# Three small reorderings in a fused spectral-mix and gated-MLP kernel with its backward pass

## The chip, the cores and the metric

One core of one Trainium2 chip. The metric is device microseconds of one launch, median of several runs. A profiled execution of the same program stands beside the runs; all durations below are from it.

## The reference, cut to what matters

Forward, with x of 2048 x 576 in bf16, F = 4608:

```python
g = sigmoid((x * gate_w).sum(-1))
a = irfft2(rfft2(x) * (w_r + 1j * w_i))              # spectral branch, over (2048, 576)
b = (gelu(x @ w_gate) * (x @ w_up)) @ w_down         # MLP branch
out = g * a + (1 - g) * b
```

Computed are `out` and, by `jax.vjp` with a given `grad_out`, the gradients of `x`, `w_r`, `w_i`, `w_gate`, `w_up`, `w_down` and `gate_w`. In the reference `x` of the MLP branch is the same array as that of the spectral branch.

## The kernel before

The 2048 rows lie as 128 partitions x 16 row tiles `t`. F is cut into 18 groups `g` of 256 columns. The main part of the kernel is a loop over `g` and over four blocks `m` of four row tiles each: 72 steps, numbered `pr = 4g + m` from 0 to 71. One step does the following on TensorE (PE), in this order:

- `H_mm`: 20 matmuls of `z = grad_out @ w_down^T` (L444, L449), the short matmuls of gate and up (L453), and then `full(0)` and `full(1)` (L460), eight matmuls for each of two pairs of row tiles. Their results lie in PSUM: `z` in the only buffer of pool `pz`, `xy` in two buffers of pool `ph`.
- ScalarE (ACT) takes `z` out (`da`, L472), then for each `xy` a square and two casts (`H_act`, L479, L481, L482). VectorE (DVE) makes the elementwise products: `H_ew1` (L487 to L491) in the same step, `H_ew2` (L507 to L528, two of them ACT sigmoids) after the next step has begun, because `sigs()` is called at the end of a step. DVE takes its instructions in this order; L528 is the last of `H_ew2`.
- the weight-gradient products of the group before: `u_dw` (d_w_gate and d_w_up, L590, 16 matmuls of 512 columns), `u_dwd` (d_w_down, L572, 16 matmuls of 288 columns) and `tail` (L604). They accumulate in the two buffers of pool `pw` and are cut into jobs of 4 or 8 matmuls. `W_units` says which jobs go to which `m`. An ACT cast (`wevac`, L541) takes a finished product out, and POOL issues its store.
- FFT pieces. The spectral branch and its gradient are cut into 207 slots (some of them empty, `gap`), held in the list `fft` in a fixed order: 64 forward pieces (`u1`: L633, L636, taken out by ACT as `Y`; `u2`: L651, taken out by ACT as `ve`, then five DVE operations and a store by SP); a table and two turned tables; then, pair by pair of rows, four 32-point pieces `s2` (L752, taken out by L757) and four `s1` (L841, L844); and the inverse pieces `z`, `ztail` (L901) and `d` (L915, L917). In the lines the first of these is L888. Every piece writes PSUM tile `pf`, and `pf` is the same single buffer of `pz` that `z` of the step uses. So a piece's first matmul waits until the piece ahead of it has been taken out, and the next step's `z` waits for the last one.

How many pieces a step gets is fixed by `want(pr)`: for the first steps by the tuple `FIRST` (running totals), after it by a share that grows evenly until the pieces are used up in step 64. When a step has pieces and its number is over 6, the first of them goes between the two row tiles of `full(1)`, that is between the gate|up halves of `xy` (L1132, `between`); the others go among the weight-gradient jobs, at places that L1154 to L1158 choose by weight. Around the first piece only, `pcopy[0]` is VectorE's copy (`VC`) in place of ScalarE's (`AC`); inverse pieces already use `pcopy[0]`, 32-point pieces do not.

A piece `s2` fills two PSUM column blocks on 128 partitions. L757 takes it out in two copies of 64 partitions x 578 elements, one for the real part (c = 0, partitions 0 to 63) and one for the imaginary part (c = 1, partitions 64 to 127). When the fourth `s2` of a pair is out, the pair's products go on DVE as "side work", about 4.4 us by the kernel's own estimate in each step, behind `H_ew1`.

The order of `dB`: `dB` holds grad_out and is scaled in place by 1 - g in four parts of four row tiles (`scale_dB`): part 0 and 2 (ACT) and 1 (DVE) in and right after step 4, part 3 (ACT, L1042) at the start of step 5's `xy`, behind the casts of two products. d_w_down uses all 16 row tiles of `dB`: its first half (`f(0)`) row tiles 0 to 7, its second row tiles 8 to 15.

After the 72 steps (from about 951 us) a second part multiplies the stored intermediates by the weights (L1276); it takes no FFT piece.

Of the kernel before, what the change touches and what calls it, by code (L numbers as in the profile page):

```python
# [19 lines left out]
S, D, DF = 2048, 576, 289  # L20
# [25 lines left out]
def eo(c):  # L46

    return slice(c, 512, 4)
# [227 lines left out]
def kernel(  # L276
# [4 lines left out]
    nc = tc.nc  # L281
# [258 lines left out]
    def wevac(out, in_):  # L540
        wcopy[0](out, in_)  # L541
# [3 lines left out]
    def dwtile(name):  # L545
        if not spare:
            return stage.tile([P, 2, FG], BF16, tag="dw", name=name)
        spare.append(spare.pop(0))
        return ew.tile([P, 4, FG], BF16, tag=spare[-1], name=name, bufs=2)[:, 0:2, :]

    def W_units(g):
        fsl = slice(g * FG, (g + 1) * FG)
        kt = kept[g]

        def tl(k, t):
            tile_ = kt[t // 4][min(k, 1)]
            return tile_[:, t % 4, :] if k == 0 else tile_[:, t % 4, k - 1, :]
        dwd_tiles, wp = {}, {}

        def halves(f, us):  # L560
            return [(us, lambda: f(0)), (us, lambda: f(1))]

        def wtile(key):
            if key not in wp:
                wp[key] = pw.tile([P, TPB, FG], F32, tag="wps", name="wps")
            return wp[key]

        def u_dwd(fch, h):
            def f(half):
                wps = wtile(("d", fch, h)).rearrange("p a b -> p (a b)")  # L570
                for t in range(8 * half, 8 * half + 8):
                    nc.tensor.matmul(wps[:, :288], lhsT=tl(0, t)[:, fch * P:(fch + 1) * P],  # L572
                                     rhs=dB[:, t, h * 288:(h + 1) * 288], start=(t == 0), stop=(t == T - 1))
                if half == 0:
                    return
                if h == 0:
                    dwd_tiles[fch] = stage.tile([P, D], BF16, tag="dwd", name="dwd")
                dwd = dwd_tiles[fch]
                wevac(dwd[:, h * 288:(h + 1) * 288], wps[:, :288])
                if h == 1:  # L580
                    r0 = g * FG + fch * P
                    wst[0].dma_start(out_6[r0:r0 + P, :], dwd[:])
            return halves(f, 1.0)

        def u_dw(c, cuts=(0, 4, 8, 12, T)):

            def f(t0, t1):
                wps = wtile(("w", c))
                for t in range(t0, t1):
                    nc.tensor.matmul(wps[:].rearrange("p a b -> p (a b)"), lhsT=xn[:, t, c * P:(c + 1) * P],  # L590
                                     rhs=kt[t // 4][1][:, t % 4].rearrange("p k f -> p (k f)"), start=(t == 0), stop=(t == T - 1))
                if t1 < T:
                    return
                dw = dwtile("dw")
                wevac(dw[:], wps[:])
                for k, ov in enumerate((o4v, o5v)):
                    wst[0].dma_start(ov[:, c, fsl], dw[:, k, :])  # L597
            return [(3.45 * (b - a) / T, lambda a=a, b=b: f(a, b)) for a, b in zip(cuts, cuts[1:])]

        def tail():  # L600
            wps = wtile("t")
            for t in range(T):
                for k, r in ((1, LO), (2, HI)):
                    nc.tensor.matmul(wps[r, 0, :], lhsT=xn[:, t, 512:576], rhs=tl(k, t),  # L604
                                     start=(t == 0), stop=(t == T - 1))
            dw = dwtile("dwt")
            wevac(dw[:, 0], wps[:, 0, :])
            wst[0].dma_start(out_4[512:576, fsl], dw[LO, 0, :])
            wst[0].dma_start(out_5[512:576, fsl], dw[HI, 0, :])
        w = [u_dw(c, (0, 12, T)) if g == 0 and c < 2 else u_dw(c) for c in range(4)]  # L610
        d = [u_dwd(fch, h) for fch in range(FCH) for h in range(2)]
        if g == 0:
            return [[w[0][:1], w[1][:1]], [d[0], d[1]], [d[2], d[3], w[2][:2]], [w[2][2:], w[3][:2]], w[3][2:], {1: [w[0][1][1], w[1][1][1]], 2: [tail]}]
        return [[d[0]], [d[1], d[2], d[3]], [w[0], w[1][:2]], [w[1][2:], w[2]], w[3], {2: [tail]}]


# [5 lines left out]
    def pftile(dt=F32):  # L622
        return pz.tile([P, 2, 512 if dt is F32 else 1024], dt, tag="z", name="pf")
# [99 lines left out]
    def mid_units():  # L723
# [13 lines left out]
        def prefetch(p):  # L737
            st[p, "vx"] = load_V(scr_x, p)
            st[p, "vg"] = load_V(scr_g, p)
            w = unit([2, 2, DF], name="Wt")  # L740
            for k, v in enumerate((A_w_r, A_w_i)):
                for sb, d in rows(w[:, k], v, p):
                    ST.dma_start(sb, d)
            st[p, "w"] = w

        def s2(p, which, j):
            def f():
                Vp = st[p, "v" + which]
                xps = pftile()
                for t in range(2):  # L750
                    g = 2 * t + j
                    nc.tensor.matmul(xps[:, t, :DF], lhsT=tb.B[:, int(p == 0 and g == 0), :], rhs=Vp[:, g, :], start=True, stop=True)  # L752
                if j == 0:
                    st[p, which] = unit([2, 2, DF], name="X" + which)
                o = st[p, which]
                for c in range(2):
                    nc.scalar.copy(o[64 * j:64 * j + 64, :, c, :], xps[64 * c:64 * c + 64, :, :DF])  # L757
                if which == "g" and j == 1:
                    side.extend(products(p))
                    if p == 0:  # L760
                        prefetch(p + 1)
            return f
# [176 lines left out]
    VC, AC = V.tensor_copy, nc.scalar.copy  # L939
    pcopy = [AC]  # L940
# [5 lines left out]
    for c in range(6):  # L946
        w = gwr[0:1, eo(c)] if c < 4 else gwr[0:1, 512:D]
# [57 lines left out]
    mid_at = 4 * T + 10  # L1005
    NPR = NT // 2
    LASTP = NG * NPR - 7
    FIRST = (0, 0, 0, 0, 0, 0, 1, 5)
    done = [0]

    def want(pr):

        n0 = FIRST[-1]
        if pr < len(FIRST):
            return FIRST[pr]

        def load(n):

            return n + 0.5 * min(max(n - mid_at, 0), n_mid)
        share = load(n0) + (load(n_slots) - load(n0)) * (pr + 1 - len(FIRST)) / (LASTP - len(FIRST))  # L1020
        n = n0
# [24 lines left out]
    for g in range(NG):  # L1046
# [3 lines left out]
        for m in range(NPR):  # L1050
# [128 lines left out]
            if done[0] == n_slots or (pr >= wgT_from and pr % 2 == 0 and len(wgT_all) < 20):  # L1179
                load_wgT()  # L1180
                if done[0] == n_slots:
                    load_wgT()
        carry = pend[4] if pend else []
        pend = W_units(g)
    flush()
    assert fft_pos[0] == len(fft) and not side
# [239 lines left out]
```

## Time and profile before

| | |
|---|---|
| median of 4 runs | 1382.4 us (1381.2 to 1383.38) |
| the profiled execution, its own time | 1381.46 us |
| its span, first to last instruction | 1379.7 us |
| VectorE busy | 781.7 us (57% of the span) |
| ScalarE busy | 701.5 us (51%) |
| L757, ScalarE, 64 copies | mean 637 ns |
| L655, ScalarE, 32 copies of `ve` | mean 660 ns |
| step 7 (81.06 to 93.03 us) | ScalarE busy 10.93 of 11.97 us |
| step 35 (447.67 to 460.34 us) | VectorE busy 10.71 of 12.67 us |

The starts of the steps are the first L444 matmul of each. Times in the text are microseconds from the span's start, or from the start of a step where that is said. A matmul's end in the profile is a model: while TensorE runs without a break, a matmul starts before the end of the one ahead of it, so lost time is read from the distance of two starts.

### The profile page before, as it was taken

The numbers are of one execution on the slowest core, as the hardware profiler recorded it, in microseconds if no ns is written. First come the engines' busy times: TensorE is split into PE (matmuls) and PEld (weight loads), VectorE is DVE, ScalarE is ACT, GpSimd is POOL, SyncE is SP. The second block draws the span as 40 slices with busy tenths as digits, with TensorE's granted clock in tenths as the row PEclk, the third lists the DMA queues.
The fourth block names the chain that finished last, engine by engine and source line by source line (L and its number), as shares of the span: only waits on it lengthen the run. The fifth ranks groups of instructions, "written<-read, shape, count | busy, mean of one in ns | idle before, by whom it ended". The sixth has DMA issues, their size and how long they took to land.

```text
span 1379.7 us, 25988 instructions
## 1 busy us (share of the span) xinstructions
PE 1363.3 (99%) x10187; PEld 910.0 (66%) x10272; DVE 781.7 (57%) x1514; ACT 701.5 (51%) x1300; POOL 262.8 (19%) x513
## 2 busy tenths in 40 slices
PE   9999999999999999999999999999999999999999
PEld 7556656566556556556656566556777777777777
DVE  7887777765988877885676766650002642122101
ACT  7887777768878777866766767651000000000000
POOL 6211111132445444331111111110000110000000
PEclk9999999999999999999999999999999999999999
DMA  7425444456566556555556656759999997788774
GB/s 234 128 86 148 123 125 120 128 163 157 133 161 167 154 159 164 132 155 150 138 155 154 166 153 162 178 126 284 196 193 202 217 193 170 154 162 164 159 149 88
DMA packets 512423, 218.94 MB, mean 159 GB/s; under 512 B 312011, under 2 KB 503181, under 8 KB 512301
## 3 DMA queue, kind: packets, MB, share of 16 engines
q1 hardware_dynamic: 495178, 191.89, 59.9%
q0 software_dynamic: 14912, 24.24, 6.2%
q8 instruction: 80, 1.31, 0.4%
q10 hardware_dynamic: 2210, 1.15, 0.3%
q14 instruction: 43, 0.34, 0.1%
HBM read 45.51 MB, written 98.30 MB: 104 GB/s over the span
## 4 chain that ended last, share of the span: by engine, by line
PE 94%; ACT 2%; DVE 2%; issue 1%; POOL 0%; ACTq 0%; DVEq 0%; POOLq 0%
PE acc L1276 31%; PE wps L590 17%; PE xy L460 17%; PE wps L572 10%; PE z L444 8%; PE wps L604 2%; PE xy L453 2%; PE z L449 2%; PE pf L633 1%; PE pf L915 1%; PE pf L841 1%; PE pf L752 1%; PE pf L917 1%; PE pf L651 1%; PE pf L636 1%
## 5 line engine op out<-in xcount | busy, mean ns | idle before, releaser
L1276 PEld LDWEIGHTS <-pin 128*128 128x128 bf16 x3456 | 338.0, 98 | 85.8 <-issue 0.5
L590 PE MATMUL wps<-dH,xn 128*128 128x512 bf16 x1136 | 270.0, 379 | 0.9
L460 PE MATMUL xy<-wgu,xT 128*128 128x512 bf16 x1083 | 258.4, 379 | 8.3 <-issue 7.0
L460 PEld LDWEIGHTS <-xT 128*128 128x128 bf16 x1152 | 106.4, 98 | 132.9 <-issue 24.8
L590 PEld LDWEIGHTS <-xn 128*128 128x128 bf16 x1152 | 111.5, 98 | 118.5 <-issue 0.6
L1293 ACT COPY bo<-acc 128x288 f32<-128x288 f32 x32 | 12.8, 399 | 305.0 <-PE acc L1276 305.0
L572 PE MATMUL wps<-dB,A 128*128 128x288 bf16 x1152 | 153.4, 286 | 0.1
L597 POOL DMA_DIRECT2D out_dram<-dw x134 | 72.8, 547 | 408.4 <-ACT dw L541 368.1
L1276 PE MATMUL acc<-wgT,pin 128*128 128x288 bf16 x1152 | 143.8, 286 | 0.0
L1276 PE MATMUL acc<-wuT,pin 128*128 128x288 bf16 x1152 | 143.6, 286 | 0.0
L1276 PE MATMUL acc<-wd_all,pin 128*128 128x288 bf16 x1152 | 142.6, 286 | 0.0
L444 PE MATMUL z<-wdT,dOT 128*128 128x256 bf16 x1152 | 137.7, 273 | 0.1
L572 PEld LDWEIGHTS <-A 128*128 128x128 bf16 x1152 | 112.1, 98 | 32.8 <-issue 0.3
L472 ACT ACTIVATE da<-z,omg 128x256 bf16<-128x256 f32 x288 | 112.0, 471 | 31.9 <-PE z L449 31.8
L444 PEld LDWEIGHTS <-dOT 128*128 128x128 bf16 x1152 | 112.4, 98 | 21.7 <-issue 0.6
L1348 DVE SCALAR_TENSOR_TENSOR f32t<-gwf,dlog,b16t 128x576 f32<-128x576 f32 x16 | 13.1, 818 | 173.3 <-DMA b16t<-dxa_scr 173.3
L481 ACT CAST xb<-xy 128x512 bf16<-128x512 f32 x144 | 85.0, 591 | 48.4 <-PE xy L460 48.4
L479 ACT ACTIVATE q<-xy 128x512 bf16<-128x512 f32 x144 | 88.0, 613 | 14.6 <-PE xy L460 13.3
L482 ACT CAST hu<-xy 128x512 bf16<-128x512 f32 x144 | 87.4, 607 | 0.0
L518 DVE TENSOR_TENSOR xb<-xb,sg 128x1024 bf16<-128x1024 bf16 x48 | 33.1, 690 | 84.8 <-ACT sg L510 84.7
L541 ACT CAST dw<-wps 128x512 bf16<-128x512 f32 x72 | 42.3, 590 | 55.5 <-PE wps L590 53.4
L1307 DVE SCALAR_TENSOR_TENSOR b16t<-b16t,g,f32t 128x576 bf16<-128x576 bf16 x16 | 13.1, 818 | 96.1 <-DMA b16t<-a_scr 95.8
(239 smaller groups left out, 1703.0 us busy)
## 6 DMA issues: line engine op xcount, KB each, us to landing
scr<-dH SPq DMA_DIRECT2D x144, 256.0 KB, 3.3
scr<-A SPq DMA_DIRECT2D x72, 256.0 KB, 2.5
out_dram<-dw POOLq DMA_DIRECT2D x134, 64.0 KB, 2.5
wd_all<-in_B_w_down_dram SPq DMA_DIRECT2D x3, 1728.0 KB
out_dram<-dwd POOLq DMA_DIRECT2D x34, 144.0 KB, 2.9
scr_p<-Vt SPq DMA_DIRECT2D x32, 145.0 KB, 2.5
wgu<-in_B_w_gate_dram SPq DMA_DIRECT2D x18, 256.0 KB, 4.3
wgu<-in_B_w_up_dram SPq DMA_DIRECT2D x18, 256.0 KB, 3.4
```

The source lines that it names most:

```text
L444: nc.tensor.matmul(zo(t), lhsT=dOT[:, ci, t, :], rhs=wdT[:, ci, :], start=(t % 4 < 2 and ci == 0), stop=False)
L460: nc.tensor.matmul(xy[k][:, t % 2, :], lhsT=xT[:, ci, t, :], rhs=wgu[:, ci, :], start=False, stop=(ci == 3))
L472: nc.scalar.activation(da[:, t, :], z[:, t % 2, t // 2, :], ACT.Copy, scale=omg32[:, 4 * m + t:4 * m + t + 1])
L479: nc.scalar.activation(q[:, h, :], xy[:, :, 0:FG], ACT.Square)
L481: nc.scalar.copy(xb[:, h, :], xy[:, :, 0:FG])
L482: nc.scalar.copy(hu[:, h, :], xy[:, :, FG:2 * FG])
L518: V.tensor_tensor(xb[:], xb[:], s[:], op=ALU.mult)
L541: wcopy[0](out, in_)
L572: nc.tensor.matmul(wps[:, :288], lhsT=tl(0, t)[:, fch * P:(fch + 1) * P], rhs=dB[:, t, h * 288:(h + 1) * 288], start=(t == 0), stop=(t == ...
L590: nc.tensor.matmul(wps[:].rearrange("p a b -> p (a b)"), lhsT=xn[:, t, c * P:(c + 1) * P], rhs=kt[t // 4][1][:, t % 4].rearrange("p k f -> ...
L597: wst[0].dma_start(ov[:, c, fsl], dw[:, k, :])
L1276: nc.tensor.matmul(acc[:, :288], lhsT=src[:, r, :], rhs=w_of(r)[:, h * 288:(h + 1) * 288], start=(first and r == 0), stop=(last and r == F ...
```

## The change

```diff
@@ W_units: jobs of group 0, by m
-            return [[w[0][:1], w[1][:1]], [d[0], d[1]], [d[2], d[3], w[2][:2]], ...
+            return [[w[0][:1], w[1][:1]], [d[0][:1], d[1][:1], d[0][1:], d[1][1:]], [d[2], d[3], w[2][:2]], ...
@@ s2: the 32-point piece
-                for c in range(2):
-                    nc.scalar.copy(o[64 * j:64 * j + 64, :, c, :], xps[64 * c:64 * c + 64, :, :DF])
+                for c, cp in enumerate((AC, pcopy[0])):
+                    cp(o[64 * j:64 * j + 64, :, c, :], xps[64 * c:64 * c + 64, :, :DF])
@@ pieces done after each of the first steps
-    FIRST = (0, 0, 0, 0, 0, 0, 1, 5)
+    FIRST = (0, 0, 0, 0, 0, 0, 1, 4, 7)
```

First, step 5, which runs the first two d_w_down products, does both first halves and then both second halves. Second, a 32-point piece that stands between the gate|up halves has its imaginary part copied by VectorE and its real part by ScalarE; elsewhere both stay on ScalarE. Third, steps 7 and 8 get three FFT pieces in place of four. As the totals after them are computed anew, the pieces of most steps up to step 60 move by one or two places: after step 8 seven pieces are done instead of nine, the totals are the same again for good from the end of step 60, and step 64 ends the list in both. No matmul is added or removed.

In the changed program 12 of the 32 `s2` pieces are the first piece of their step (steps 25, 26, 27, 30, 32, 33, 35, 36, 38, 39, 41 and 44). In steps 7 and 8 the order of TensorE's matmuls becomes, by line and count (without L444 to L453; L633 and L636 are one `u1`, L651 is one `u2`):

```
step 7 before  L460x12 u1 L460x4 L590x4 u2 L590x4 u1 L590x4 u2 L590x4
step 7 after   L460x12 u1 L460x4 L590x4 u2 L590x8 u1 L590x4
step 8 before  L460x12 u1 L460x4 L590x4 u2 L590x4 u1 L572x8 u2 L572x8
step 8 after   L460x12 u2 L460x4 L590x4 u1 L590x4 L572x8 u2 L572x8
```

More of the change, by code (lines that the diff above doesn't have):

```diff
@@ L612, in W_units @@
         if g == 0:
-            return [[w[0][:1], w[1][:1]], [d[0], d[1]], [d[2], d[3], w[2][:2]], [w[2][2:], w[3][:2]], w[3][2:], {1: [w[0][1][1], w[1][1][1]], 2: [tail]}]
+            return [[w[0][:1], w[1][:1]], [d[0][:1], d[1][:1], d[0][1:], d[1][1:]], [d[2], d[3], w[2][:2]], [w[2][2:], w[3][:2]], w[3][2:], {1: [w[0][1][1], w[1][1][1]], 2: [tail]}]
         return [[d[0]], [d[1], d[2], d[3]], [w[0], w[1][:2]], [w[1][2:], w[2]], w[3], {2: [tail]}]
```

## The prediction

> **What bounds the kernel now.** I read the page's busy times first, then the chain that ended last, TensorE's waits, and the timeline around each wait.
>
> ```profile
> PE 1363.3 (99%) x10187; PEld 910.0 (66%) x10272; DVE 781.7 (57%) x1514; ACT 701.5 (51%) x1300; POOL 262.8 (19%) x513
> ...
> PE 94%; ACT 2%; DVE 2%; issue 1%; POOL 0%; ACTq 0%; DVEq 0%; POOLq 0%
> ```
>
> TensorE (PE) is the bound from start to end, and the change adds and removes no matmul. So only time in which PE stands still can move. PE's own list of waits names what the change can reach:
>
> ```profile
> PE pf L633 <- ACT ve L655: 0.9, 2, 0.6
> PE pf L752 <- ACT Xg L757: 0.5, 1, 0.5
> ```
>
> (Total, times, longest.) Both are the single `pf` buffer: a piece waits until ScalarE has taken out the one ahead. The list hides waits shorter than the modelled end of a matmul, so I measure lost time by distances of starts. Undisturbed, four L590 matmuls take 0.86 us to the next start, eight take 1.72, eight L572 take 0.98. Step 7, from the timeline (start, duration, engine, line, operation; in brackets the idle time before it and what ended it), first TensorE's rows, then one of ScalarE's:
>
> ```profile
> 87.64 1.03 PE L590 MATMUL wps<-dH,xn 128*128 128x512 bf16 x4
> 88.50 0.41 PE L651 MATMUL pf<-Y,Rt 128*128 128x292 bf16 x2
> 88.75 1.02 PE L590 MATMUL wps<-dH,xn 128*128 128x512 bf16 x4
> 90.42 0.42 PE L633 MATMUL pf<-Dt,xT 128*128 128x146 bf16 x4 [0.64 <-ACT ve L655]
> ...
> 89.66 0.70 ACT L655 COPY ve<-pf 128x584 f32<-128x584 f32 x1
> ```
>
> The first two rows give 0.86. From 88.75 to 90.42 it is 1.67: 0.81 lost, because ScalarE, busy almost without a break since 77.6, reaches `ve` at 89.66 only. TensorE goes on at 90.42, 0.06 after the copy's end. The same reading over steps 5 to 71:
>
> - step 5: 32 L572 matmuls last 4.37; 16 last 2.12 and 16 more 1.96, so 0.29 lost. The second half of the first d_w_down product waits for the last part of `dB` (ScalarE L1042, 62.03 to 64.84; TensorE goes on at 64.89).
> - step 7: 0.81, and 0.09 before its last `u2`; step 8: 0.39 (100.71 to 101.96 with four L590).
> - step 35: eight L590, 455.95 to 458.37, 2.42 against 1.72: 0.69. Steps 26, 38, 44: 0.2 each.
> - steps 14, 18, 54, 59: 0.14, 0.26, 0.09, 0.14, lone places where four L590 are too short a cover for a copy. Steps 13, 16, 18, 19, 22: together 0.6, which stay.
>
> That is 4.1 us in all, the ceiling of any gain.
>
> **The change part by part, costed on TensorE.**
>
> (1) *d_w_down by halves.* No instruction more. The first half of the second product (8 x L572, 0.98 us) now covers the wait of 0.29. Its PSUM buffer is free by 62.2 (L541 casts, 61.09 to 62.18), before its start at about 63.7. Both products still finish at the step's end and are cast in the same place. **-0.3.** ScalarE, late in steps 5 to 7, does not eat this gain: in step 6 it waits for TensorE itself (0.36 us before its cast at 77.57), so all after it starts earlier too.
>
> (2) *One piece less in steps 7 and 8.* Step 7: between the first `u2` and the next `u1` now stand eight L590, 1.72 us, and `ve` is out 1.67 after their start: no wait. The last `u2` and its 0.09 leave. Step 8: order u2, u1, u2. Its first copy keeps ScalarE's place of `Y` (99.00, 0.67), the `u1` follows, and behind it stand four L590 and eight L572, 1.84 us, over a copy of 0.65. **-0.8 - 0.1 - 0.4 = -1.3.** The moved pieces' 0.4 to 0.7 us of matmul are paid in later steps. Each carries its DVE work (2.0 us for a `u2`, into steps with 2 to 4 us of idle VectorE) and one SP store a step later (2.2 us to landing). The table, the loads `Vp` (5.3 to 5.9 us) and POOL's twelve `Wt` issues (0.5 us each) shift with them. The first 32-point piece moves from 317.6 to about 325 and its loads from about 297 to about 305, some 20 us ahead of use: no cost, and one only if more than 14 us of that cover went.
>
> (3) *32-point copies.* ScalarE loses 12 copies of 0.64. VectorE gets 12 of 64 x 578 from PSUM, of which the trace has none. Bounds: VectorE's cast of 288 elements, 0.45, and of 1024, 1.22. I take 0.76, the nearest row (L925, 580 elements, 757 ns). In the changed program VectorE's copy waits for ScalarE's counter alone, so it stands behind the ScalarE half, not beside it. It also stands behind L528 on VectorE. Behind it wait `H_ew1` and the side work; nothing on TensorE needs these soon (`dH` is read a group later). Step 35:
>
> ```profile
> 453.79 1.28 ACT L757 CAST Xx<-pf 64x578 bf16<-64x578 f32 x2
> ...
> 454.28 0.69 DVE L528 TENSOR_TENSOR dH<-dH,sg 128x1024 bf16<-128x1024 bf16 x1
> ...
> 455.70 0.41 PE L752 MATMUL pf<-Vp,Btab 128*128 128x289 bf16 x2
> ...
> 457.01 1.31 ACT L757 CAST Xg<-pf 64x578 bf16<-64x578 f32 x2
> ...
> 458.37 0.41 PE L752 MATMUL pf<-Vp,Btab 128*128 128x289 bf16 x2 [0.52 <-ACT Xg L757]
> ```
>
> ScalarE's half ends at 454.43, L528 at 454.97, VectorE's half at 455.73; TensorE wants 455.70 and gets 455.79: +0.09. In return ScalarE's next copies end 0.64 earlier, 457.68, just as TensorE wants them: -0.69. Steps 26 and 44 likewise (-0.2 each); in 38 the next piece gets 12 L590 of cover (-0.2). At 0.45 the 0.09 is gone. At 1.22 it is 0.55, and step 39 could lose as much, 1.0 more in all. In the other ten steps L528 ends 6.3 to 7.8 after the step's start and the next piece is wanted at 8.0 to 9.9, so 0.76 fits. **-1.2.**
>
> A copy of 580 elements out of PSUM takes 757 ns on VectorE (L925) and 658 on ScalarE (L923). The Trainium skill, "Perfetto Trace Analysis", section "Optimizing Scalar/DVE Operations", has a rule that speaks against this part: VectorE's access overhead is about 125 ns on PSUM, ScalarE's about 51. The trace agrees in sign. By the page a moved copy would take, as an estimate, 0.07 us more than ScalarE's, and the sum would differ by under 0.1, since only step 35 has no slack.
>
> (4) *The shifted schedule, steps 14 to 60.* Gone with their neighbours: 0.14 + 0.26 + 0.09 + 0.14 = -0.6. New short covers, read from the new order:
> - step 21 becomes like step 13 (u1, then u2 after eight L572, then u1): 166.45 to 167.58 against 0.98, +0.15; step 17 about +0.05.
> - step 52 puts a `d` four L590 after a wide `z`. As in step 60 the `z` copy (1.01) would start 0.65 after the first L888, at 771.05, and end at 772.06; the `d` would be wanted at 770.85 + 0.86 = 771.71: +0.41.
> - step 60 starts with a `z` copied by VectorE, and the `d` follows after four L590, not eight as in step 56:
>
> ```profile
> 723.71 0.69 DVE L528 TENSOR_TENSOR dH<-dH,s 128x1024 bf16<-128x1024 bf16 x1
> 724.32 1.22 DVE L891 CAST ZT<-pf 128x1024 bf16<-128x1024 f32 x1
> ...
> 724.35 1.89 PE L590 MATMUL wps<-dH,xn 128*128 128x512 bf16 x8
> ```
>
> Wanted at 724.35 + 0.86 = 725.21, free at 725.54 + 0.06: +0.39. Together **-0.6 + 1.0 = +0.4.** I add 0.3 for short covers I may have missed (two of the kind of step 13).
>
> Sum: -0.3 - 1.3 - 1.2 + 0.4 + 0.3 = **-2.1 us**. The profiled execution took 1381.46 (span 1379.7, 1.76 around it) and would take 1379.4; it lies 0.94 below the median of the runs shown, to which I apply the same difference: 1382.4 - 2.1 = **1380.3 us**.
>
> **The rivals.**
> - *Full gain.* Every wait named goes, and the new ones of (4) are hidden (a copy starting earlier because ScalarE runs ahead): -0.3 - 1.3 - 1.3 - 0.6 = -3.5, 1378.9 us. For it: ScalarE idles 2 to 5 us in steps 52 and 60. Against it: those waits are one copy's own length, which idle time doesn't shorten.
> - *Only moved.* The pieces pushed out of steps 7 and 8 make as many short covers as they leave: the new schedule has seven steps with five pieces (13, 17, 21, 52, 56, 60, 64), the old one six, one of them with empty slots. Then -0.3 - 1.3 - 1.2 is answered by some 2.5 of new waits: 1382.1 us. For it: fifteen steps lost time before, 0.1 to 0.9 each, at places that the weights in the source do not tell.
> - *VectorE late (slower).* In steps 28, 29, 33 and 43 VectorE idles 0.4 to 0.6 us of 12 to 13, and in step 28 L528 ends 8.06 after the start. If its queue were that late in all 12 steps, TensorE would stand (8.06 + 0.76 + 0.06 - 8.04) = 0.84 in each: +10.1, with the rest 1382.4 - 2.1 + 10.1 = 1390.4. It decides once these waits add up to more than 2.1, that is from 0.18 a step. Against it: step 28 itself starts with an `s1`, and the 12 steps have L528 at 6.1 to 7.8.
>
> **How the numbers follow.** Forecast 0.56, full gain 0.24, only moved 0.14, VectorE late 0.06. The forecast's own range is 1379.3 to 1381.3 (the unknown copy's 1.0 upwards, (4)'s 1.0 of new waits downwards). For 8 in 10 I take 1378.3 to 1382.7: full gain and only-moved included, with the runs' own spread about a median; VectorE late is left out. 0.2%, about what a measurement of this kernel can tell from no change, is 2.8 us: faster means below 1379.6, slower above 1385.2. Full gain is faster, and a little of the forecast's lower end (0.05): 0.29. Slower is VectorE late, 0.06. The rest, 0.65, is within.
>
> **What would show it.** Right: `pf L633 <- ACT ve L655` gone from TensorE's waits, no L572 row in step 5 ending late, step 35's last L752 0.7 us nearer the one ahead; L757 on VectorE x12 of about 0.76 us; new waits at L915 in steps 52 and 60. Wrong: L752 waiting on VectorE for over 0.2 us in several steps, waits of `pf` on a DMA, or the second part of the kernel (from about 951) changing its length.

## The result and the profile after

The changed kernel takes 1379.43 us (median; before in the same comparison 1381.32). The ratio is 0.9987, 95% interval 0.9982 to 0.9991: 1.9 us or 0.14% less. The interval leaves out 1, so the kernel is faster, but by less than the 0.2% that the prediction took for the bound of "faster". The spans of the profiled executions differ by 2.1 us (1379.7 to 1377.6): 2.04 in the part from step 5 to the second part, 0.19 in the part ahead of it, which varies from execution to execution, and 0.14 the other way behind the last matmul. The absolute number, 1380.3, was 0.9 too high because it hung on a median of four runs; the median of many lies 1.1 us lower.

The page of after, its busy times and its chain:

```profile
PE 1361.7 (99%) x10186; PEld 909.2 (66%) x10272; DVE 789.0 (57%) x1526; ACT 694.3 (50%) x1288; POOL 262.2 (19%) x513
...
PE 95%; DVE 2%; DMA 1%; issue 1%; ACT 0%; ACTq 0%; SPq 0%; DVEq 0%
```

TensorE is still the bound; ScalarE lost 7 us of work and VectorE took as much. TensorE's list of waits in after (total, times, longest):

```profile
PE xy L460 <- issue: 7.0, 44, 0.2
...
PE pf L915 <- ACT ZT L891: 0.2, 1, 0.2
PE pf L915 <- DVE ZT L891: 0.2, 1, 0.2
```

The two `pf` rows of before (L633 and L752) are gone, and two new ones stand at L915. (A third new row, L415 with 0.6, lies at about 6 us, ahead of the first step.) Step 7 in the timeline of after (start, duration, engine, line, operation):

```profile
88.02 0.41 PE L651 MATMUL pf<-Y,Rt 128*128 128x292 bf16 x2
...
88.27 1.89 PE L590 MATMUL wps<-dH,xn 128*128 128x512 bf16 x8
...
89.19 0.70 ACT L655 COPY ve<-pf 128x584 f32<-128x584 f32 x1
...
90.00 0.42 PE L633 MATMUL pf<-Dt,xT 128*128 128x146 bf16 x4
```

From 88.27 to 90.00 it is 1.73, the undisturbed length of eight L590: the 0.81 is gone. The copy ends at 89.89, 0.11 before the next piece starts. The eight L590 are the *cover* of that copy: the matmuls that run while the buffer is being emptied. In step 8 a new wait stands:

```profile
100.99 0.41 PE L651 MATMUL pf<-Y,Rt 128*128 128x292 bf16 x2
...
101.24 1.14 PE L572 MATMUL wps<-dB,A 128*128 128x288 bf16 x8
...
101.78 0.65 ACT L655 COPY ve<-pf 128x584 f32<-128x584 f32 x1 [0.98 <-PE pf L651]
...
102.47 1.80 PE L444 MATMUL z<-wdT,dOT 128*128 128x256 bf16 x15
```

Eight L572 give 0.98 to the next start, and the next step's `z` comes after 1.23: 0.25 lost. The copy starts 0.79 after L651 did; where ScalarE is idle, its other copies start 0.45 to 0.5 after. VectorE's copies, from the view of the line L757 (duration min/median/max in ns, first and last start):

```profile
L757 ACT CAST Xx<-pf x27: 635/637/639, 323.9 to 558.2; 64x578 bf16<-64x578 f32 x27
L757 ACT CAST Xg<-pf x25: 635/637/638, 328.9 to 569.0; 64x578 bf16<-64x578 f32 x25
L757 DVE CAST Xg<-pf x7: 754/762/764, 339.3 to 566.0; 64x578 bf16<-64x578 f32 x7
...
L757 DVE CAST Xx<-pf x5: 754/762/764, 324.6 to 527.3; 64x578 bf16<-64x578 f32 x5
```

Twelve copies of 0.762, against 0.76 taken. The Trainium skill, "Perfetto Trace Analysis", "Optimizing Scalar/DVE Operations", agrees in sign, but the row gives a difference of 0.125 us to ScalarE's copy where its figures gave an estimate of 0.07. Those figures are busy times; the same section puts the profiled latency at about twice them, and by that the estimate would be 0.15. Step 35 in after:

```profile
451.59 0.64 ACT L757 CAST Xx<-pf 64x578 bf16<-64x578 f32 x1
...
451.72 0.69 DVE L528 TENSOR_TENSOR dH<-dH,sg 128x1024 bf16<-128x1024 bf16 x1
...
452.33 0.75 DVE L757 CAST Xx<-pf 64x578 bf16<-64x578 f32 x1
...
453.64 0.41 PE L752 MATMUL pf<-Vp,Btab 128*128 128x289 bf16 x2
...
453.84 0.58 ACT L541 CAST dw<-wps 128x512 bf16<-128x512 f32 x1 [0.16 <-PE wps L590]
453.89 1.89 PE L590 MATMUL wps<-dH,xn 128*128 128x512 bf16 x8
...
454.45 1.28 ACT L757 CAST Xx<-pf 64x578 bf16<-64x578 f32 x2
...
455.78 0.41 PE L752 MATMUL pf<-Vp,Btab 128*128 128x289 bf16 x2
```

VectorE's half stands behind L528, as said, and is out at 453.08, 0.56 before the second L752: no wait there. The third L752 comes 1.89 after the eight L590 began (455.78 - 453.89): 0.17 lost. Between the second piece and its copies ScalarE makes the cast L541 of a finished product. Step 26 has the same order on ScalarE, and the next step's `z` comes 0.17 late:

```profile
342.67 0.58 ACT L541 CAST dw<-wps 128x512 bf16<-128x512 f32 x1 [0.44 <-PE wps L590]
...
343.28 1.28 ACT L757 CAST Xx<-pf 64x578 bf16<-64x578 f32 x2
```

And step 60:

```profile
775.36 0.69 DVE L528 TENSOR_TENSOR dH<-dH,s 128x1024 bf16<-128x1024 bf16 x1
...
775.97 1.22 DVE L891 CAST ZT<-pf 128x1024 bf16<-128x1024 f32 x1
776.00 1.03 PE L590 MATMUL wps<-dH,xn 128*128 128x512 bf16 x4
...
777.23 0.22 PE L915 MATMUL pf<-Dt,ZT 128*128 128x145 bf16 x1 [0.21 <-DVE ZT L891]
```

1.23 for four L590 of 0.86: 0.37 lost, where 0.39 had been worked out.

The time lost on TensorE, by distances of starts, in us (steps 13, 16, 19, 22 and the second place of 18 keep their 0.07 to 0.16):

| place | before | foreseen | after |
|---|---|---|---|
| 5, second half of d_w_down | 0.29 | 0 | 0 |
| 7, `u1` behind `ve` | 0.81 | 0 | 0 |
| 7, last piece | 0.09 | 0 | 0.09 (ahead of step 8's `z`) |
| 8 | 0.39 | 0 | 0.25 (ahead of step 9's `z`) |
| 14, 18, 54, 59 | 0.63 | 0 | 0 |
| 21; 17 | 0 | 0.15; 0.05 | 0.16; 0 |
| 26; 38; 44 | 0.2 each | 0 | 0.17; 0; 0 |
| 35 | 0.69 | 0.09 | 0.17 |
| 52; 60 | 0 | 0.41; 0.39 | 0.40; 0.375 |
| all of these | 3.5 | 1.1 + 0.3 for missed ones | 1.6 |

The measure for all that follows is the *stretch* from the first L444 of step 5 to the first L1276: 896.73 us before, 894.68 after, -2.04 (-1.89 in the table, the rest at places under 0.05). Equal stretches of TensorE's work repeat within 0.01 us between executions: steps 61 to 70 do in before and after, and the second part takes 424.66 from its first to its last matmul in all twelve profiles. The part ahead of step 5, which waits for loads, varies by up to 0.5, and what follows the last matmul takes 3.40 to 3.56, 0.14 more in after than in before; why is not known. The prediction had named a change of the second part's length as a sign against itself; on TensorE there is none. That is how a difference can be read that the times don't resolve, though each stretch is read from one profiled execution.

### The profile page after: what moved, and what is told of

It reads as the page before. It is cut to its first block, busy times and chain, and to the rows that moved or that the text cites. A ratio compares the mean times of both kernels' runs of the same rounds, so it can differ in the third digit from the quotient of the medians.

```text
span 1377.6 us, 25978 instructions
## 1 busy us (share of the span) xinstructions
PE 1361.7 (99%) x10186; PEld 909.2 (66%) x10272; DVE 789.0 (57%) x1526; ACT 694.3 (50%) x1288; POOL 262.2 (19%) x513
## 4 chain that ended last, share of the span: by engine, by line
PE 95%; DVE 2%; DMA 1%; issue 1%; ACT 0%; ACTq 0%; SPq 0%; DVEq 0%
PE acc L1276 31%; PE wps L590 18%; PE xy L460 17%; PE wps L572 10%; PE z L444 8%; PE wps L604 2%; PE xy L453 2%; PE z L449 2%; DMA wgu<-in_B_w_up_dram 1%; PE pf L633 1%; PE pf L915 1%; PE pf L651 1%; PE pf L752 1%; DMA xn<-in_A_x_dram 1%; PE pf L917 1%
## 5 line engine op out<-in xcount | busy, mean ns | idle before, releaser
L1276 PEld LDWEIGHTS <-pin 128*128 128x128 bf16 x3456 | 338.0, 98 | 85.8 <-issue 0.5
L590 PE MATMUL wps<-dH,xn 128*128 128x512 bf16 x1135 | 269.6, 379 | 1.0
L460 PE MATMUL xy<-wgu,xT 128*128 128x512 bf16 x1083 | 258.3, 379 | 8.3 <-issue 7.0
L460 PEld LDWEIGHTS <-xT 128*128 128x128 bf16 x1152 | 106.4, 98 | 132.6 <-issue 24.8
L590 PEld LDWEIGHTS <-xn 128*128 128x128 bf16 x1152 | 111.7, 98 | 119.0 <-issue 0.6
L572 PE MATMUL wps<-dB,A 128*128 128x288 bf16 x1152 | 153.7, 286 | 0.0
L1276 PE MATMUL acc<-wgT,pin 128*128 128x288 bf16 x1152 | 143.8, 286 | 0.0
L1276 PE MATMUL acc<-wuT,pin 128*128 128x288 bf16 x1152 | 143.6, 286 | 0.0
L1276 PE MATMUL acc<-wd_all,pin 128*128 128x288 bf16 x1152 | 142.6, 286 | 0.0
L444 PE MATMUL z<-wdT,dOT 128*128 128x256 bf16 x1152 | 137.7, 273 | 0.1
L572 PEld LDWEIGHTS <-A 128*128 128x128 bf16 x1152 | 112.1, 98 | 32.9
L444 PEld LDWEIGHTS <-dOT 128*128 128x128 bf16 x1152 | 112.4, 98 | 21.9 <-issue 0.9
L482 ACT CAST hu<-xy 128x512 bf16<-128x512 f32 x144 | 87.4, 607 | 0.0
L541 ACT CAST dw<-wps 128x512 bf16<-128x512 f32 x72 | 42.3, 589 | 53.3 <-PE wps L590 50.2
```

The source lines that it names most:

```text
L444: nc.tensor.matmul(zo(t), lhsT=dOT[:, ci, t, :], rhs=wdT[:, ci, :], start=(t % 4 < 2 and ci == 0), stop=False)
L460: nc.tensor.matmul(xy[k][:, t % 2, :], lhsT=xT[:, ci, t, :], rhs=wgu[:, ci, :], start=False, stop=(ci == 3))
L482: nc.scalar.copy(hu[:, h, :], xy[:, :, FG:2 * FG])
L1276: nc.tensor.matmul(acc[:, :288], lhsT=src[:, r, :], rhs=w_of(r)[:, h * 288:(h + 1) * 288], start=(first and r == 0), stop=(last and r == F ...
```

## The experiments

**The three parts, each alone.** Each is the kernel before with one hunk of the change.

```diff
+ [d[0][:1], d[1][:1], d[0][1:], d[1][1:]]            # e1
+ FIRST = (0, 0, 0, 0, 0, 0, 1, 4, 7)                 # e2
+ for c, cp in enumerate((AC, pcopy[0])): cp(...)     # e3
```

> The kernel before with the reordered first d_w_down products alone. Account by TensorE's waits: the loss of 0.29 us at 64.89 (32 L572 in 4.37 us) is gone, everything behind it starts 0.3 earlier, from step 5 to the second part 896.7 - 0.3 = 896.4 us, and step 7 still loses 0.81. Rival (ScalarE is the real bound of steps 5 to 7 and gives nothing back): step 7's wait grows by the same 0.3 and the stretch stays at 896.7.

Measured: 1380.94 us, ratio 0.9997 (0.9988 to 1.0006), stretch 896.47: -0.26. Timeline of this run, step 5:

```profile
61.84 2.81 ACT L1042 ACTIVATE dB<-dB,omg 128x576 bf16<-128x576 bf16 x4
...
62.57 4.08 PE L572 MATMUL wps<-dB,A 128*128 128x288 bf16 x32
...
66.49 1.25 PE L444 MATMUL z<-wdT,dOT 128*128 128x256 bf16 x10
```

`dB`'s last part ends at 64.65, as late as before within the step, but the 32 L572 now last 4.08, not 4.37. Step 7 keeps its 0.81 to 0.01: ScalarE, late there, did not eat the gain.

> The kernel before with the new totals of pieces (three in steps 7 and 8) alone, all 32-point copies on ScalarE. Account by waits: step 7's 0.81 and step 8's 0.39 go, 0.25 comes back ahead of step 9, the shift costs +0.3 (step 52 0.40, step 60 0.38, less the short covers of 14, 18, 54, 59), and the third L752 of step 35 still loses about 0.7, others 0.2: the stretch from step 5 to the second part is 0.3 to 0.8 us shorter than 896.7. Rival (only moved): no shorter at all. Rival (the pieces do all of it): 1.7 or more shorter, as with the whole change.

Measured: 1380.82 us, 0.9995 (0.9986 to 1.0004), stretch 896.28: -0.44. Steps 7 and 8 as in after, 52 and 60 with 0.40 and 0.38. With copies on ScalarE alone the new order also loses 0.21, 0.21 and 0.25 in steps 30, 32 and 39, 0.205 in 26 and 0.70 in 35.

> The kernel before with the imaginary half of a 32-point piece on VectorE where the piece is first in its step, alone (11 copies). Account by waits: step 35's 0.69 becomes about 0.17, the 0.2 of steps 26, 38 and 44 go, steps 7 and 8 keep 0.81 and 0.39: the stretch is 0.9 to 1.2 us shorter than 896.7. Rival (VectorE late): new waits of L752 or L841 on VectorE, 0.2 or more in several steps, and a stretch no shorter.

Measured: 1380.19 us, 0.9991 (0.9983 to 1.0), stretch 895.65: -1.08. Step 35 goes from 0.69 to 0.11, lost at the second L752: VectorE's half lasts from 454.99 to 455.76 and TensorE goes on at 455.81. Steps 26 and 44 are free but for 0.05 ahead of step 27, and 0.17 stands ahead of step 39.

The three make -0.26 - 0.44 - 1.08 = -1.78; together they give -2.04. So the parts don't simply add up: VectorE's half is worth 1.08 in the old order and 1.3 in the new one (894.68 against 896.28, less the 0.29 of step 5). In the new order it also covers the 0.66 of steps 30, 32 and 39. But it has nothing to gain in steps 38 and 44, whose 0.2 each are gone with the new order alone, and less in step 26, where 0.17 stays.

**Both halves on VectorE.** The changed kernel, with the pieces between the gate|up halves copied by VectorE alone.

```diff
-                for c, cp in enumerate((AC, pcopy[0])):
+                for c, cp in enumerate((pcopy[0], pcopy[0])):
```

> The changed kernel with both halves of a 32-point piece on VectorE where it is first in its step: the suspected cost doubled, 12 x 2 copies of 0.76. Account by waits: the pair ends at L528's end + 1.5, and TensorE waits only where that is later than the next piece is wanted: steps 32 (0.2), 35 (0.3), 36 and 41 (0.1 each), 0.7 us in all, up to 2 if the fuller VectorE drifts late in steps 27 to 35. So the stretch from step 5 to the second part is 894.7 + 0.4 to 2.0. Rival (VectorE late decides): about 0.8 in each of the 12 steps, +9 or more, slower than the kernel before. Rival (VectorE's copies are free): no change against 894.7, and then step 35 gains 0.2 more as ScalarE is emptier.

Measured: 1380.1 us, 0.9991 (0.9982 to 1.0) to before, stretch 895.45: 0.77 more than after. Its step 35 in the timeline:

```profile
451.93 0.69 DVE L528 TENSOR_TENSOR dH<-dH,sg 128x1024 bf16<-128x1024 bf16 x1
...
452.65 1.53 DVE L757 CAST Xx<-pf 64x578 bf16<-64x578 f32 x2
...
454.24 0.42 PE L752 MATMUL pf<-Vp,Btab 128*128 128x289 bf16 x2 [0.23 <-DVE Xx L757]
```

1.53 of VectorE behind L528 is too much there (0.40), and in steps 32, 36 and 41 (0.21, 0.15, 0.13); the other steps lose nothing by it. Behind L528, VectorE can be a little late, and is not late in every step.

**The old totals from step 49.** The changed kernel, with steps 50 to 60 in the order of before.

```diff
+        k0, n0 = (8, 5) if pr > 48 else (len(FIRST), n0)
-        share = ... (pr + 1 - len(FIRST)) / (LASTP - len(FIRST))
+        share = ... (pr + 1 - k0) / (LASTP - k0)
```

> The changed kernel, with the number of pieces done by the end of each step taken from the old rule from step 49 on, so that steps 50 to 60 have the order of before and steps 0 to 48 that of after. Theory (part 4 of the prediction: the new waits at L915 are short covers of this order alone): the 0.40 of step 52 and the 0.375 of step 60 go, the 0.09 of step 54 and the 0.14 of step 59 come back, so the stretch from step 5 to the first L1276 falls from 894.68 us to 894.1 (-0.55), and the kernel takes 1378.9. Rival (the waits at L915 come from ScalarE or VectorE running late since the 32-point pieces): both stay in some form, stretch 894.5 to 895.0.

Measured: 1378.8 us, ratio to before 0.9984 (0.9975 to 0.9993), stretch 894.14: -0.54. Steps 52 and 60 are free; 54 and 59 lose their old 0.09 and 0.14. The waits at L915 belong to the order of the pieces, not to a late engine.

**Four pieces in step 8.** The changed kernel, with three in step 9.

```diff
-            return FIRST[pr]
+            return FIRST[pr] + (pr == 8)
```

> The changed kernel with four pieces in step 8 (u2, u1, u2, u1) and three in step 9, all else in the order of after. It asks what the piece taken out of step 8 is worth once step 7 has only three. Theory of the prediction (step 8 had too short a cover of its own): the Y copy after the first u1, 0.72, and then L541, 0.58, stand ahead of the ve copy, so about 0.18 is lost ahead of the second u2 and 0.15 ahead of the second u1, while the 0.25 ahead of step 9 goes: the stretch is 894.68 + 0.1 = 894.8 (894.6 to 895.0). Rival (step 8's loss of 0.39 was only what ScalarE had carried over from step 7): no wait in step 8, stretch 894.4.

Measured (one execution, as in the next two experiments): stretch 894.86, +0.18; 0.17 lost ahead of the second `u2`, 0.25 ahead of the second `u1`, where 0.15 was expected. There the third `ve` copy again starts 0.78 after L651, 0.16 after ScalarE was free, so its delay doesn't come from a long idle time ahead of it. The rival falls: step 8's cover is too short by itself for four pieces. But three in place of four save only 0.17.

**An early touch of `ve`.** The changed kernel, with one copy more, of 128x1 into the third `ve`, which is overwritten; for it `ve` is taken from its pool ahead of the two matmuls.

```diff
+                if (src is xT) and t == 2:
+                    nc.scalar.copy(ve[:, 0, 0:1], omg32[:, 0:1])
```

> The changed kernel with one ScalarE copy of 128x1 into the third ve buffer ahead of the two L651 that end step 8; it takes over the wait for GpSimd's counter, so that the ve copy waits for TensorE's counter and for ScalarE's own. Theory A (the copy starts 0.32 late because of the second counter, whichever): the 0.25 ahead of step 9 stays, stretch 894.7. Theory B (it is GpSimd's counter that costs): the copy starts some 0.05 after TensorE's counter, the 0.25 goes, stretch 894.4. In both the 128x1 copy itself lies beside matmuls and costs nothing.

Measured: stretch 894.45, -0.24. The end of step 8 in its timeline:

```profile
100.79 0.20 ACT L651 COPY ve<-omg 128x1 f32<-128x1 f32 x1
...
101.09 0.41 PE L653 MATMUL pf<-Y,Rt 128*128 128x292 bf16 x2
...
101.34 1.14 PE L572 MATMUL wps<-dB,A 128*128 128x288 bf16 x8
...
101.59 0.65 ACT L655 COPY ve<-pf 128x584 f32<-128x584 f32 x1 [0.61 <-PE pf L653]
...
102.32 0.49 PE L444 MATMUL z<-wdT,dOT 128*128 128x256 bf16 x3
```

(The matmul has moved to line 653.) The copy now starts 0.50 after its matmuls, not 0.79, ends at 102.24, and `z` comes 0.98 after the eight L572 began. So the 0.25 came from the late start, and the late start went when the small copy took over the wait for GpSimd's counter, though GpSimd had last raised that counter 60 us earlier, at 41.8 in after. The copy still waits for two counters, TensorE's and ScalarE's own, and that costs nothing. But the small copy is also the first to write this buffer, and it moves the copy one place back in ScalarE's queue; no run tells these apart from the counter.

**The cast behind the piece's copy**, in steps 26 and 35 of the changed kernel.

```diff
+                def fin(): ...                           # L541 and its stores
+                late.append(fin) if hold[0] else fin()   # in u_dw; hold[0]: pr in (26, 35)
+                    while late: late.pop(0)()            # in the loop over jobs, after the piece
```

> The changed kernel with ScalarE's cast of a finished weight gradient (L541, 0.58) put behind the copy of the piece that follows the product, in steps 26 and 35 alone. Theory (what was left in these steps, 0.17 ahead of step 27 and 0.17 ahead of step 35's third piece, is this cast standing between the piece and its copy of 1.28): the copy starts 0.45 after L752 and ends at 1.73, the buffer is wanted at 1.97: both waits go, stretch 894.34. Rival (eight L590 are too short for two copies of 0.64 whatever stands ahead): both stay at 0.1 to 0.17, stretch 894.6 to 894.7.

Measured: stretch 894.36, -0.32; both waits gone. Step 35 in its timeline:

```profile
453.75 0.41 PE L752 MATMUL pf<-Vp,Btab 128*128 128x289 bf16 x2
...
454.00 1.89 PE L590 MATMUL wps<-dH,xn 128*128 128x512 bf16 x8
454.19 1.29 ACT L757 CAST Xx<-pf 64x578 bf16<-64x578 f32 x2 [0.41 <-PE pf L752]
...
455.50 0.59 ACT L541 CAST dw<-wps 128x512 bf16<-128x512 f32 x1
...
455.72 0.41 PE L752 MATMUL pf<-Vp,Btab 128*128 128x289 bf16 x2
```

The copies start 0.44 after L752, not 0.81, and eight L590 take 1.72 again.

**The mended versions.** The last three edits together, and then the cast behind the copy in every step (`hold[0]`: `pr > 6`).

> The changed kernel with the three edits together that each took away a wait of its own: the old totals from step 49, the 128x1 copy that takes the wait for GpSimd's counter out of step 8, and the cast put behind the piece's copy in steps 26 and 35. If the waits are independent, the stretch is 894.68 - 0.54 - 0.24 - 0.32 = 893.6 us and the time about 1378.3. Rival (one wait taken away brings another behind it, as when the parts of the change were run alone): more than 893.8.

Measured: 1378.31 us, ratio to before 0.9977 (0.9968 to 0.9986), stretch 893.60. The waits were independent.

> The kernel of the run before with the cast of a finished weight gradient behind the piece's copy in every step from 7 on. Theory (a cast of 0.58 ahead of a copy matters only where the cover is short, and only steps 26 and 35 had lost time by it): no difference, 893.6. Rival (a PSUM buffer of the products that comes free 0.6 to 1.3 later makes TensorE wait ahead of a later L590, or stores that start later do): 0.2 or more longer.

Measured: 1378.03 us, 0.9975 (0.9965 to 0.9984), stretch 893.47: 0.13 less than the run ahead, so neither was quite right. Nothing waits for a later buffer, and the 0.09 of step 54, which the old totals had brought back, goes too: there as well a cast had stood ahead of a copy. The other 0.04 is in step 43. This is the fastest of all, 3.3 us under before. Some 1.0 us of lost time remains in steps 7 to 59, none over 0.16 at a place. TensorE's list of waits in it has no row left from step 5 on:

```profile
PE pf L944 <- POOL ident masks.py:199: 1.4, 1, 1.4
PE pf L423 <- DVE par_i L112: 0.4, 1, 0.4
PE pf L399 <- DVE dOT L406: 0.2, 1, 0.2
```

## Why the prediction was right, and where it was not

The sum, -2.1, is close to what was measured (-2.04 in the stretch, -1.9 in the medians), and the likeliest case held: old waits go, named new ones come. That the sum agrees so well is in part luck: four places lost 0.6 more than foreseen, which the 0.3 put in for missed covers met in part, and some 0.15 went at places under 0.05 that the prediction had not counted. By its parts:

1. *d_w_down by halves*: -0.3 foreseen, -0.29 measured (-0.26 alone).
2. *One piece less in steps 7 and 8*: -1.3 foreseen, -0.94 measured. Step 7's 0.81 went whole. The 0.09 of its last `u2` moved to the last `u1`, which has the same four L590 over its copy. In step 8 the prediction gave a cover to the `u1` and none of its words to the last `u2`. By its own copy it fits in eight L572, as the early touch shows; in after the copy began 0.29 later than there. In before, the third `ve` copy came straight behind a cast (L482, 100.76 to 101.36), so this could not show.
3. *32-point copies*: -1.2 foreseen, -0.96 measured at the four places named. The unknown duration was taken right. Of the 0.96, the 0.4 of steps 38 and 44 would have gone with the new order alone; for step 44 the prediction gave that gain to VectorE's half. The +0.09 at step 35's second piece is right for the old order (0.11, copies alone) and nothing in the new one, where VectorE's L528 of step 35 starts 6.1 us after the step's start, not 6.6. What stays is the 0.17 in steps 26 and 35. The step that failed is "ScalarE's next copies end 0.64 earlier ... just as TensorE wants them": ScalarE, freed, did reach the place early, found its cast L541 first in the queue, waited for TensorE there (0.16 and 0.44) and began the copies only behind it. The run with the cast behind the copy shows it: both 0.17 go.
4. *The shifted schedule*: +0.4 foreseen, +0.31 measured: -0.63, and 0.16 + 0.40 + 0.375. Step 17's 0.05 wasn't there.

In place of the 0.3 for missed covers came 0.6: 0.25 ahead of step 9, 0.17 ahead of step 27, 0.09 ahead of step 8 and 0.08 in step 35. The second and the last are no short covers but an instruction ahead in ScalarE's queue.

Of the rivals, *full gain* fails on the waits at L915: they are one copy's length over a short cover, as was said against it. *Only moved* names a true thing (1.2 us of waits are new, at the end of step 8 and in steps 21, 52 and 60) of too small a size. *VectorE late* needed waits of 0.18 or more in each of the 12 steps; after has no such wait, and even twice the work on VectorE cost 0.77.

## What to carry to other kernels

Where one PSUM buffer hands over from piece to piece, write the next order out and compare each cover (distance of two starts) with the copy over it; that found three of the new waits to 0.02 us from the profile before. Then look at what stands in the copying engine's queue between the piece and its copy: where the cover is short, a cast that itself waits for TensorE there is lost time (0.17 in steps 26 and 35, 0.09 in step 54), and putting it behind the copy cost nothing. A gain early in a schedule that shares out work evenly moves the later places too, and it pays to hold those where they were good (0.54 here).

## What the runs showed of the hardware

A ScalarE copy that waited for TensorE's and for GpSimd's counter began 0.29 us later than the same copy waiting for TensorE's and its own, though GpSimd's value had been reached 60 us before. It is alone: of the ScalarE instructions in after that sat idle for TensorE's counter, it began 0.36 after that counter's update (or after ScalarE was free, if that was later), and every other within 0.08. Whether the cost lies in GpSimd's counter, in the first use of the buffer or in that place of the queue stays open: an earlier copy that waited for the same two counters, L640 at 90.77 in after, started 0.51 after its matmuls.

The row "PE xy L460 <- issue: 7.0, 44, 0.2" is no wait. The last run's profile holds all 10272 matmuls, after's only 10186, and with the full records the row is gone while the stretch changed by what the other rows say:

```profile
PE 1370.4 (100%) x10272; PEld 909.4 (66%) x10272; DVE 789.8 (57%) x1526; ACT 693.8 (50%) x1289; POOL 262.6 (19%) x513
```
